# A new stored order for the 1722 operations of an attention and gMLP kernel

## The chip, the core and the metric

One of the eight cores of a Trainium2 chip runs the whole program. A core has five engines, each with a queue of its own that it works through strictly in order: PE (TensorE, the matrix multiplier), ACT (ScalarE, activations), DVE (VectorE), POOL (GpSimd) and SP (SyncE, which here only issues DMAs). An engine that reaches an instruction whose inputs are not ready waits, and everything behind that instruction on the same engine waits with it. The metric is the device time of one execution in microseconds (us); lower is better.

## What is computed

The reference takes x (2048 rows of 448 numbers, bf16) and applies two blocks, each with a residual and with a modulation that comes from a vector c:

```
sa, ca, ga, sb, cb, gb = (silu(c) @ w_mod) cut into six
h = layernorm(x) * (1 + ca) + sa
x = x + ga * A(h)
h = layernorm(x) * (1 + cb) + sb
x = x + gb * B(h)
```

A is causal attention with 16 heads of 28 and a window of 256 rows, then a projection with wo. B is a gated MLP: z = gelu(h @ w_in) is halved into z1 and z2 (896 columns each); z2 is normalised over its columns and mixed over all 2048 rows, g = w_sp @ layernorm(z2) + b_sp; the result is (z1 * g) @ w_out.

## The kernel before, in words

**Tiles.** The 2048 rows are 16 tiles of 128, called t or j. Attention runs per tile j over the up to three key tiles kb = j-2, j, j-1, in two halves each, so that there are 90 pairs of a score block and its exponential.

**Operations.** The program is a list of 1722 operations, each made once by a helper (`pe`, `dve`, `pool`, `load`, lines 438 to 448) with its inputs, the buffers that it touches and the engines that may run it. The names that the prediction uses are:

- load and norm of x: `l1_t` is the statistics of tile t (st, ag, ve on DVE, line 588 to 595), `l1_trs` the power of minus one half on POOL (line 596), `xn` the normalised tile (lines 609, 610, 639), `tr` its transpose on PE, `hT` or `hm` the modulation that gives the transposed h (lines 672, 677, 686). `modA` and `modAe` make the modulation's columns (line 573), and `zv` and `zqk` are memsets on POOL that clear rows of weights (lines 526, 527).
- projections: `qk` and `v` on PE, with `qke` (line 785 on DVE, 782 on ACT) and `ve` (797, 794) which copy the result out of PSUM.
- attention: `S` the scores on PE, `E` the exponential on ACT (line 884), `M` the mask on POOL (line 890), `PV` on PE, then `oq`, `rec`, `nrm`, `oT` (lines 916 to 925; oq, rec and oT on DVE, nrm on either of two engines), `wo` on PE and `x1` on DVE (line 935, the residual).
- second norm: `l2_t` and `x2` as `l1` and `xn`, `h2T` a transpose by DMA, `h2m` its modulation (line 686; four of them, c = 0 to 3, serve two tiles, and what reads h waits for all four).
- block B: `z2m` and `z1m` on PE, `z2g` and `z1g` the gelu on ACT (988, 992, 1011), `l3` the statistics of z2, `z2n` its norm on DVE (line 610), `wsp` a transposing DMA of a piece of w_sp, `G` the mixing over rows on PE in four quarters of four matmuls with 512 columns each, `ga` and `gu` on DVE (1080, 1082), `out` on PE, `fin` the last residual on DVE (1102) and `st` the store (1104).

**Order and waits.** The order is not found when the kernel is built. It stands in the text `ORDER` from line 177, one token for an operation: its number, after a dot which of its possible engines runs it, and after a slash which buffers (PSUM banks, SBUF slots) its new tensors get. `schedule` reads the tokens:

```python
        for tok in ORDER.split():
            head, _, picks = tok.partition("/")
            num, _, opt = head.partition(".")
            o = self.ops[int(num)]
            ...
                    t.got = t.options[picks.pop(0)]
            ...
            o.eng, _, o.fn = o.opts[int(opt or 0)]
            ...
            self.order.append(o)
```

So the order of the tokens of one engine is the order of that engine's queue. A buffer that is used again makes its new user wait for all users of the old tensor. `emit` then writes each queue with the semaphore waits that the inputs and the reused buffers demand; the order between engines comes from these waits alone. `column_tiles` looks at runs of certain PE operations: those that stand next to a column-tiled one are themselves run as four matmuls of 32 columns (line 453 in place of line 456).

**The PSUM banks.** There are eight. The scores use three pairs (0 and 1, 2 and 3, 4 and 5) in the early part, and the rest of attention works with banks 4 to 7 one at a time; a projection, a wo or a z2m that takes a bank waits until DVE or ACT has emptied it. In block B all eight banks are in use.

Of the kernel before, what the change touches and what calls it, by code (L numbers as in the profile page):

```python
# [177 lines left out]
22 23 1 0 33 32 3 19 26 1700/0 20 30 1701 21 31 34/0 35 36 1702 1703 1704 1705 2 5 6 62 63 24 64 25 65 66/1 71/7 69/0 73/6 1706 1707 9 37/2 38 39 40  # L178
41 29.1 13 42 43 4 67/3 44 45 1708 1709 1710 46 47 48 49 50 51 52 53 72 1711 1712 1713 1714 1715 1716 60.2 70.1 74 1717 120 121 122 123 85/2 1718 68.1
175 61.1 75/6 76 90/0 91 10 124 177 54.2 1719 1720 1721 110/5 111 86 87 80/4 92 93 176 77 57.1 78 178 56.1 79.1 58 88 81 82 83 179 125.2/4 128/1 94 89  # L180
126/0 112 59 113 84 491/0,0 129 160/1 161 12 8 17 127.1 162 150/0 151 152 114 140/3 141 180 493/8 155/2 142 156 157 163 164 240 55.2 16 143 244 181
242 246 153 154 183.2/4 100/0 101 95/2 102 103 96 97 98 105/3 158 159 243 245 104 241 130/1 131 132 133 134 182.1/2 184/0 106 185 99 247 144 248 249
28.1 186.1 323 250 251/3 254.1/0 11 145/2 146 147 148 149 327 107 108 109 252.1/1 329 135/1 136 137 328 138 139 492/0,0 496/0 494 115/1 116 7 117 118
119 165/2 166 167 168 170/0 171 187/3 169 188 508/1,0 253.1/2 325 512/7 189.1 172 173 174.1 489/2 513 200/3 201 202 203 15 509/1 510 204 190/1 191 192
193 194 210/0 515/1,0 516/4 518/3 195/3 27 211 212 213 326 220/1 221 222 223 14 490 205/2 206 207 208 209 214.1 495/0 497 224.1 498 196 330 324 331
499/0 500 215/1 216 217 18 408 332 255 218 219 529/0,1 530/8 235/0 197 198 533/0 258 199.1 409 225/2 226 227 228 229.1 501.1/0 256 257 261.1 236 237
238 333 262 259 260 230/3 239 231 232 233 536/1,0 514/0 511 234 335/2 537/9 406 407 263/2 264 265 283/3 284 540/10 336.1/1 531 303/1 266 267 285 286
# [984 lines left out]
```

## Time and profile before

Three runs gave 271.55, 272.40 and 272.97 us, so a median of 272.40 us. The profiled execution took 271.84 us, of which the trace's span is 270.1 us; the other 1.7 us lie around it.

| | busy us | share of the span |
|---|---|---|
| PE, matmuls | 257.9 | 95% |
| PE, weight loads (beside the matmuls) | 127.5 | 47% |
| DVE | 175.4 | 65% |
| ACT | 132.9 | 49% |
| POOL | 98.6 | 37% |

The granted TensorE clock is full in every slice of the profile. The time falls into four stretches: the start (0 to about 17 us: loads, the modulation, the first norm and projections); attention (to about 108 us, the last scores), in which ACT works through the 90 exponentials while PE does scores, PV, projections and the first of block B; the rest of z1 and z2 (to about 147 us); and the dense stretch, in which PE does G and out, to the last store.

A line of the chain of waits names a time in us, a length, an engine and what it did; it is followed back from the last instruction. A group line ends with the idle time of the engine ahead of that group, and who ended it.

### The profile page before, as it was taken

Reading aid. Unit: us, or ns where it says so; the run is one execution under the profiler, and the core shown is the slowest. Engines: PE = TensorE matmul, PEld = TensorE weight load, DVE = VectorE, ACT = ScalarE, POOL = GpSimd, SP = SyncE. Lnnn points to the kernel's source line nnn. Section 1 sums busy time; section 2 is a strip of 40 time slices with the busy share of each in tenths; the row PEclk is TensorE's granted clock in tenths of the full one; section 3 lists DMA queues with packets and bytes.
Section 4 is the critical chain, followed back from the end, with each engine's and each line's share of the span. In section 5 each row is a group of like instructions: output and inputs, shape, how many; then the busy total and the mean of one; then the engine's idle time right before and its main releaser. Section 6 shows DMA issues by size and latency. Waiting matters only on the chain.

```text
span 270.1 us, 7271 instructions
## 1 busy us (share of the span) xinstructions
PE 257.9 (95%) x3128; PEld 127.5 (47%) x3149; DVE 175.4 (65%) x414; ACT 132.9 (49%) x180; POOL 98.6 (37%) x158
## 2 busy tenths in 40 slices
PE   6889999999999989999999999999999999999995
PEld 2657444554455443454444444444444444444453
DVE  3899798978989989698987944341334233332443
ACT  4789999999999998967687200001000000000000
POOL 3577377766888678753731210000000000000000
PEclk9999999999999999999999999999999999999999
DMA  7975335350579851957699990000000000000013
GB/s 226 379 176 55 65 86 90 98 136 4 127 107 221 119 80 22 157 100 156 134 152 188 194 175 21 0 0 2 0 0 0 2 0 34 34 2 34 17 51 106
DMA packets 60862, 23.97 MB, mean 89 GB/s; under 512 B 49822, under 2 KB 60701, under 8 KB 60829
## 3 DMA queue, kind: packets, MB, share of 16 engines
q1 hardware_dynamic: 60555, 23.03, 41.9%
q8 instruction: 25, 0.41, 0.6%
q10 hardware_dynamic: 274, 0.46, 0.5%
q14 instruction: 8, 0.07, 0.1%
HBM read 9.59 MB, written 1.84 MB: 42 GB/s over the span
## 4 chain that ended last, share of the span: by engine, by line
PE 77%; DVE 15%; DMA 3%; issue 1%; ACT 1%; POOL 1%; DVEq 0%; ACTq 0%; SPq 0%
PE ps L456 71%; PE ps L453 6%; DVE st_all L588 2%; DVE QKT L785 2%; DVE oq L916 2%; DMA wmod_sb<-in_w_mod_dram 2%; DVE w_out_sb L940 1%; DVE oT L925 1%; DMA out_dram<-fin 1%; DVE hT L686 1%; DVE x_sb L935 1%; DVE z L982 1%; ACT PT L884 1%; DVE o_sb L921 1%; DVE mv_all L591 1%
## 5 line engine op out<-in xcount | busy, mean ns | idle before, releaser
L884 ACT ACTIVATE PT<-ps 128x1024 bf16<-128x1024 f32 x90 | 85.0, 1038 | 3.3 <-PE ps L456 3.0
L1080 DVE TENSOR_TENSOR tmpg<-ps,bsp_bc 128x512 bf16<-128x512 f32 x28 | 19.4, 692 | 59.7 <-PE ps L456 56.8
L456 PE MATMUL ps<-QKT,z 128*128 128x512 bf16 x218 | 49.9, 379 | 0.3
L890 POOL TENSOR_SCALAR_AFFINE_SELECT PT<-PT 128x512 f32<-128x512 f32 x60 | 37.0, 638 | 10.5 <-ACT PT L884 10.4
L1011 ACT ACTIVATE z1T<-ps 128x512 bf16<-128x512 f32 x28 | 15.1, 596 | 39.1 <-PE ps L456 39.0
L456 PEld LDWEIGHTS ps<-QKT,z 128*128 128x128 bf16 x224 | 21.8, 98 | 26.4 <-ACT z2raw L992 0.4
L596 POOL TENSOR_TENSOR rs_all<-ve_all,neghalf 128x1 f32<-128x1 f32 (+2 forms) x30 | 20.1, 673 | 32.6 <-DVE ve_all L595 32.5
L456 PE MATMUL ps<-w_spC,z 128*128 128x512 bf16 x111 | 25.4, 379 | 0.1
L456 PE MATMUL ps<-w_spD,z 128*128 128x512 bf16 x110 | 24.7, 379 | 0.1
L456 PE MATMUL ps<-w_out_sb,z1T 128*128 128x448 bf16 (+2 forms) x119 | 22.3, 341 | 0.1
L456 PE MATMUL ps<-w_in_sb,hT 128*128 128x448 bf16 (+1 forms) x101 | 22.0, 353 | 0.0
L456 PE MATMUL ps<-hT,w_in_sb 128*128 128x512 bf16 (+1 forms) x87 | 20.9, 380 | 0.5 <-ACT z1T L1011 0.2
L588 DVE BATCH_NORM_STATS2 st_all<-z2raw 128x6 f32<-128x448 bf16 x32 | 18.7, 613 | 1.4 <-ACT z2raw L992 0.8
L588 DVE BATCH_NORM_STATS2 st_all<-x_sb 128x6 f32<-128x448 bf16 x32 | 19.2, 612 | 0.5 <-DMA x_sb<-in_A_x_dram 0.3
L456 PE MATMUL ps<-hT,WQK 128*128 128x128 bf16 (+2 forms) x109 | 18.2, 295 | 1.3 <-DVE oq L916 0.3
L456 PE MATMUL ps<-QKT 28*128 28x128 bf16 x720 | 18.3, 217 | 0.8 <-DVE hT L677 0.5
L785 DVE CAST QKT<-ps 128x512 bf16<-128x512 f32 (+2 forms) x26 | 16.1, 623 | 3.5 <-PE ps L456 2.4
L609 POOL TENSOR_SCALAR xn<-x_sb,rs_all,nm_all 128x512 bf16<-128x512 bf16 x20 | 15.7, 787 | 4.1 <-DVE nm_all L600 3.1
L456 PEld LDWEIGHTS ps<-w_spC,z 128*128 128x128 bf16 x112 | 10.9, 98 | 13.2 <-ACT z2raw L992 0.2
L456 PEld LDWEIGHTS ps<-w_spD,z 128*128 128x128 bf16 x112 | 11.0, 98 | 13.0
L456 PEld LDWEIGHTS ps<-QKT 28*128 28x128 bf16 x720 | 10.4, 92 | 13.9 <-ACT PT L884 10.1
L456 PEld LDWEIGHTS ps<-w_out_sb,z1T 128*128 128x128 bf16 x119 | 11.5, 98 | 10.1 <-DVE z1T L1082 0.4
(90 smaller groups left out, 331.8 us busy)
## 6 DMA issues: line engine op xcount, KB each, us to landing
wmod_sb<-in_w_mod_dram SPq DMA_DIRECT2D x8, 224.0 KB, 3.6
w_in_sb<-in_B_w_in_dram SPq DMA_DIRECT2D x8, 224.0 KB, 2.9
out_dram<-fin SPq DMA_DIRECT2D x16, 112.0 KB, 1.7
x_sb<-in_A_x_dram SPq DMA_DIRECT2D x3, 448.0 KB, 7.3
wqk_raw<-in_A_wqkv_dram SPq DMA_DIRECT2D x2, 452.0 KB, 6.0
bsp_bc<-in_B_b_sp_dram SPq DMA_DIRECT2D x1, 512.0 KB, 6.2
wmod_sb<-in_w_mod_dram SPq DMA_DIRECT2D x1, 448.0 KB, 4.9
wmod_sb<-in_w_mod_dram ACTq DMA_DIRECT2D x1, 448.0 KB, 5.0
```

The lines of the kernel that those rows point to most:

```text
L453: last = e.matmul(out_[32 * j:32 * j + 32], lhsT=lhsT[:, 32 * j:32 * j + 32], rhs=rhs, start=st, stop=sp, tile_position=(0, 32 * j), **kw)
L456: return e.matmul(out_, lhsT=lhsT, rhs=rhs, start=st, stop=sp, **kw)
L588: st = [dve("%sst%d" % (name, i), prio, dve_ns(D), lambda e, i=i, s_=s_: e.bn_stats(st_all[:, slot, t, i, :], s_()), deps, tens) for i, s_ ...
L591: return dve(name + "ag", prio, 100, lambda e: e.bn_aggr(mv_all[:, slot, t, :], st_all[:, slot, t, 0:n, :]), st)
L596: r = pool(name + "rs", prio, 420 + 148 * n, lambda e: e.tensor_tensor(rs_all[:, slot, t0:t1], ve_all[:, slot, t0:t1], neghalf[:, t0:t1], ...
L609: return e.tensor_scalar(dst, src, rs_all[:, slot, t:t + 1], nm_all[:, slot, t:t + 1], ALU.mult, ALU.add)
L785: return e.tensor_copy(QKT[:, g, cols], ps[:, ten.slot, 0:w])
L884: e_op = P.op("E%d_%d" % (j, ui), pr, [("act", 925, lambda e, e_in=e_in, e_out=e_out: e.activation(e_out(), e_in(), ACT.Exp, scale=SCALE)) ...
L890: ready = pool("M%d_%d" % (j, ui), pr - 50, pool_ns(512), lambda e, pt=pt, pat=pat, cm=cm, cmp=cmp: e.affine_select(out=pt32(pt.slot), in_ ...
L916: tq = dve("oq%d" % j, pr - 10, dve_ns(512), lambda e, pv_ten=pv_ten, qt=qt: e.transpose(out=oq[:, qt.slot, :], in_=ps[:, pv_ten.slot, :]) ...
L1011: g = P.op("z1g%d_%d" % (tb, ft), pr - 19, [("act", act_ns(512), lambda e: e.activation(z1T[:, ft, tb * 512:(tb + 1) * 512], ps[:, ten.slo ...
L1080: a = dve("ga%d_%d" % (tb, ft), pr, dve_ns(512), lambda e, tb=tb, ten=ten, tg=tg: e.tensor_tensor(tmpg[:, tg.slot, :], ps[:, ten.slot, :], ...
```

## The change

Only the text `ORDER` changes. The operations, their inputs and the code that reads the order stay as they are; line numbers behind the text go up by one, since the new text is one line longer. It was found by a search that replays the order with assumed durations, in three versions, two of which disturb the durations and the DMA latencies.

```diff
 ORDER = """
-22 23 1 0 33 32 3 19 26 1700/0 20 30 1701 21 31 34/0 35 36 1702 1703 1704 1705 2 5 6 62 63 24 64 25 65 66/1 71/7 69/0 73/6 1706 1707 9 37/2 38 39 40
...
-1566 1567/3 1568 1675/3 1676 1677 1678 1679/3 1680 1635/2 1636 1637/0 1638 1573/3 1574 1575/0 1576 1685/2 1686 1687/3 1688 1578 1689/7 1690 1691/2
-1681/2 1682 1683/0 1623/5 1624 1625/1 1684 1692 1696/0 1697 1626 1693/4 1694 1698/3 1695 1699 1579/2 1580 1569/5 1570 1571/0 1572
+13 23 20 31 0 33 1 26 22 32 3 30 34/0 35 19 1700/0 25 1701 21 1702 1703 36 1704 62 63 1705 24 64 65 2 5 6 61.1 1706 1707 9 66/0 73/3 69/6 67/0 71/4
...
+1690 1691/2 1568 1577/7 1578 1579/1 1580 1685/4 1686 1692 1687/1 1688 1696/6 1697 1698/3 1693/1 1573/2 1574 1575/2 1576 1694 1695 1699 1569/0 1570
+1571/0 1572
 """
```

Read through the list of operations, it does this. Forty operations change their engine: 21 go from DVE to POOL (among them hm4_0, hm4_3, hm5_0, hm5_3, nrm1, nrm5, x2_0, x2_11 and ten of the h2m), 10 from POOL to DVE (nrm7, nrm8, x2_9, x2_12 and others), 4 from ACT to DVE (hT0_2, qke2_5, qke3_2, ve4), 4 from DVE to ACT (hT0_0, hT0_1, hT2_1, z2e4_1), 1 from ACT to POOL. DVE has 400 operations where it had 411, POOL 166 where it had 154, ACT 175 where it had 176 (two of them DMAs); PE 871 and SP 110 in both. The waits in the five queues go from 961 to 957. Column-tiled operations go from 246 to 250, and PE's changes of tile shape from 120 to 119. On PE the scores keep their order and their distance from each other: ahead of each S up to S15_4 stands the same PE work within half a microsecond. Within that the queues are reordered in hundreds of places. The places that the prediction speaks of, as they stand in the queues (an engine in brackets where the operation moved there):

```
POOL, start
 before  wqkf0_0  l1_2rs  wqkf0_1  xn2  l1_4rs  zv  xn7
 after   wqkf0_0  wqkf0_1  xn2  zv  l1_4rs  xn7
DVE, start
 before  xn0  zwp  modAe  hT0_1  l1_1st0  l1_1ag  l1_1ve  hT0_0  l1_2st0
 after   xn0  l1_1st0  l1_1ag  modAe  l1_1ve  hT0_2  l1_2st0
DVE, before v10 on PE
 before  qke4_2  hm5_0  hm5_2  x1_5  qke4_7
 after   qke4_2  hm5_2  rec6  x1_5  qke4_7            (hm5_0 is on POOL)
DVE, before qk5_1 and wo7 on PE
 before  qke5_5  l2_5st0  l2_2nm  x2_0  qke5_3  x1_6  l2_6st0  qke5_1  oT7  l2_4st0  l2_4ag  l2_5ag  qke5_0
 after   qke5_5  qke5_3  l2_4ve  x1_6  qke5_1  oT7  l2_6st0  qke5_0
DVE, second norm of tiles 12 and 13
 before  oq14 rec14 nrm14 h2m8_2 oT14 l2_12st0 l2_12ag l2_13ag l2_12ve z2e4_0 ... x1_14
 after   oq14 l3_7st1 l2_13st0 rec14 nrm14 l2_12ag l3_7st0 oT14 z2e4_0 x1_14 l2_13ag l2_12ve
POOL, the same
 before  M15_3  l2_12rs  x2_13  l3_7rs
 after   M15_3  l2_12rs  h2m8_1  h2m8_0  h2m10_2  h2m10_0  x2_13  h2m10_1  h2m10_3
last outs on PE
 before  ... out13  out7  out14  out12  out8  outh15  out15  out5
 after   ... out4  out12  out14  out7  out13  outh15  out15  out6  out5
slots of the four fin buffers that the last fins take, and whose store must have landed first
 before  fin7 takes that of fin14 (st14), fin5 that of fin12 (st12)
 after   fin13 takes that of fin7 (st7), fin6 that of fin14 (st14), fin5 that of fin12 (st12)
```

SP's queue changes too: wv0, one half of the v weights, is the 8th load on it and was the 13th, and the 32 wsp pieces come in another order (10 of them ahead of h2T15, where it was 14).

113 lines of the change are left out of this document (57 added, 56 removed).

## The prediction

> **What bounds the kernel now.** I read the page first (busy times, slices), then the busy time by stretch, then the chain of waits in order of time, and last the timelines of single engines around each gap of the chain. On the page, the digits are tenths of a fortieth of the span.
>
> ```profile
> span 270.1 us, 7271 instructions
> PE 257.9 (95%) x3128; PEld 127.5 (47%) x3149; DVE 175.4 (65%) x414; ACT 132.9 (49%) x180; POOL 98.6 (37%) x158
> ACT  4789999999999998967687200001000000000000
> L884 ACT ACTIVATE PT<-ps 128x1024 bf16<-128x1024 f32 x90 | 85.0, 1038 | 3.3 <-PE ps L456 3.0
> ```
>
> PE is busy nearly everywhere, but a busy PE in the trace is not yet a full one, so I look at who is full beside it. ACT is at nine tenths or more from 20 to 105 us: there it sets the pace with its 90 exponentials, and all that it could still give is the 3.3 us that it stood idle ahead of them, 3.0 of them for PE. After attention ACT empties and PE alone counts:
>
> ```profile
> 70.00:80.00 10.00, 9.41 (x251) 4.99 (x251) 9.08 (x22) 9.71 (x12) 8.94 (x15) 1.00 0.75 110
> 160.00:170.00 10.00, 9.95 (x47) 4.54 (x47) 4.64 (x8) 0.00 (x0) 0.00 (x0) 1.00 0.22 44
> ```
>
> (Columns: PE, weight loads, DVE, ACT, POOL, granted clock, DMA share, GB/s.) From 160 us on PE lacks 0.05 us in ten. The chain shows the same stretch as matmuls end to end, and PE's timeline the last of them:
>
> ```profile
> 162.74 10.74 PE ps L456 x49
> ```
>
> ```profile
> 255.43 11.34 PE L456 MATMUL ps<-w_out_sb,z1T 128*128 128x448 bf16 x66
> ```
>
> 49 matmuls in 10.74 us are 0.219 us each, and the last one ends at 266.77. The amount of PE work is the same before and after, so the dense stretch cannot become shorter; it can only begin earlier or later, or get holes. The end is thus: the time at which PE leaves attention, plus a constant, plus holes in what follows, plus the tail behind the last matmul. The sum goes by these four.
>
> **Term 1, the start: -0.45 us.** The columns below are start, length, engine and line; the bracket is the idle time ahead of it and its releaser.
>
> ```profile
> 7.85 0.17 DVE L573 TENSOR_TENSOR modT<-ps,zero_one 128x8 f32<-128x8 f32 x1 [2.23 <-PE ps L456]
> 8.38 0.62 DVE L588 BATCH_NORM_STATS2 st_all<-x_sb 128x6 f32<-128x448 bf16 x1
> 16.36 0.29 PE L456 MATMUL ps<-QKT 28*128 28x128 bf16 x8 [0.54 <-DVE hT L677]
> 16.91 0.93 PE L456 MATMUL ps<-wv_sb,hT 128*128 128x448 bf16 x4 [0.27 <-POOL wv_sb L526]
> 15.43 1.01 POOL L596 TENSOR_TENSOR rs_all<-ve_all,neghalf 128x4 f32<-128x4 f32 x1 [0.76 <-DVE ve_all L595]
> 16.39 0.46 POOL L526 MEMSET wv_sb<- 64x448 bf16 x1
> ```
>
> The v projection starts at 16.91 because zv ends at 16.85, and zv starts late only because it stands behind l1_4rs (1.01 us). In the new order it stands ahead of that, right after xn2; POOL was idle for 0.76 there, in which its 0.46 fits. So v0 follows the scores S0_0h2 directly, which end at 16.65, and 0.27 of idle PE go. S0_0h2 itself waits 0.54 for hT2_0 on DVE, which has as many statistics ahead of it as before; a little comes of the rest of the start, and I give it 0.1. Behind v0, hT2_1 leaves DVE, where v1 and gateA were ahead of it in time and qk2 on PE waited on, for ACT:
>
> ```profile
> 19.17 1.02 ACT L884 ACTIVATE PT<-ps 128x1024 bf16<-128x1024 f32 x1 [0.57 <-PE ps L456]
> ```
>
> ACT was idle for 0.57 ahead of this exponential, E1_1, so hT2_1, shorter than an exponential, costs it 0.4 at most and mostly nothing. For qk2's earlier start I give 0.08. That makes 0.27 + 0.1 + 0.08 = 0.45. A loss stands against this: modAe (the 7.85 row) is now behind the statistics of tile 1 (the 8.38 row), whose x must have landed.
>
> ```profile
> x_sb<-in_A_x_dram SPq DMA_DIRECT2D x2, 112.0 KB, 3.8
> DMA to landing us min/median/max: 2.0/6.2/8.3
> ```
>
> ```profile
> 9.40 0.32 DVE hT L677
> ```
>
> The two 112 KB loads have a median of 3.8 us and the shortest is 2.0, so the second takes some 5.6; issued some 2.2 us after the start (SP's fourth issue) it lands at 7.8. Statistics (0.62) and their aggregate come first, so modAe ends near 8.77 in place of 8.02: 0.75 late. Before, the last of the four hT0 ended at 9.72 (the 9.40 row), behind these same statistics on DVE. Now one is on DVE and three on ACT, one after the other, from 8.8: at 0.3 to 0.4 each the last ends near 9.95. So the first projections lose some 0.25, and the wait for hT2_0 at 16.36 swallows it. Ends for this term: -0.9 (the 0.54, the 0.27 and the 0.1) and +0.5 (0.75 less 0.25, if nothing swallows it).
>
> **Term 2, attention: -0.7 us.** Two of the chain's stalls on DVE lie where ACT was waiting for scores.
>
> ```profile
> 56.76 0.25 DVE rec_all L917
> ```
>
> ```profile
> 59.82 1.33 DVE hT L686 x2
> 61.15 0.54 DVE x_sb L935
> ```
>
> ```profile
> 69.63 0.53 DVE st_all L588
> 70.16 0.06 DVE nm_all L600
> 70.22 0.67 DVE xn L609
> 70.89 0.61 DVE QKT L785
> 71.54 0.83 PE ps L453 x12
> ```
>
> In the first, v10 on PE waits for x1_5 (61.15) to empty its bank, and that stands behind hm5_0 and hm5_2, 1.33 us for the two. hm5_0 goes to POOL and rec6 comes in (a reciprocal took 0.25): x1_5 is ready 1.33/2 - 0.25 = 0.41 us sooner. In the second, qk5_1 (the 71.54 row) waits for qke5_3 (70.89), and between qke5_5 and qke5_3 stand l2_5st0, l2_2nm and x2_0, 0.53 + 0.06 + 0.67 = 1.26 us, all gone from there. What PE has to gain stands in the list of waits (total, times, longest):
>
> ```profile
> PE ps L456 <- DVE x_sb L935: 0.6, 2, 0.3
> ...
> PE ps L453 <- DVE QKT L785: 0.4, 2, 0.3
> ```
>
> One of each is here: 0.3 + 0.3 = 0.6. Whether time comes of it depends on ACT:
>
> ```profile
> 63.62 8.75 ACT L884 ACTIVATE PT<-ps 128x1024 bf16<-128x1024 f32 x9 [0.20 <-PE ps L456]
> 72.54 1.94 ACT L884 ACTIVATE PT<-ps 128x1024 bf16<-128x1024 f32 x2 [0.17 <-PE ps L456]
> ```
>
> ```profile
> 103.08 3.93 ACT L884 ACTIVATE PT<-ps 128x1024 bf16<-128x1024 f32 x4 [0.57 <-PE ps L456]
> 107.52 1.02 ACT L884 ACTIVATE PT<-ps 128x1024 bf16<-128x1024 f32 x1 [0.51 <-PE ps L456]
> ```
>
> Two exponentials in a row take 1.94, one alone 1.04 (the group's mean), so they start 0.90 apart. Nine at that pace take 8 x 0.90 + 1.04 = 8.24; the row at 63.62 takes 8.75, so 0.51 lie inside it, and with 0.20 and 0.17 ahead ACT has 0.88 to give. Between PE's 0.6 and ACT's 0.88 I take 0.7. The 0.57 and 0.51 at the end of attention stay: PE has the same work between the scores there. Ends: 0 and -3.3 (the whole idle time of the group).
>
> POOL gets hm5_0, hm5_3, nrm5 and x2_0 between 55 and 80 us and gives up nrm7: three operations more, at most 1.01 each (the longest POOL row above), where it has 8.94 of ten in the second half. I cost that at +0.2, as a mask is needed only when its PV comes, behind the next scores; without that cover it costs up to 3.0.
>
> **Term 3, from attention to the last matmul: +0.2 us.** Here PE had no gap over 0.2, and I see none closing. It can get one: l2_12ve now stands behind x1_14 on DVE, and on POOL l2_12rs, which waits for it, has h2m8_1 and h2m8_0 behind it, without which z2m9 cannot start.
>
> ```profile
> 116.15 1.32 PE ps L453 x24
> ```
>
> ```profile
> 115.67 0.70 POOL L596 TENSOR_TENSOR rs_all<-ve_all,neghalf 128x2 f32<-128x2 f32 x1 [2.61 <-DVE ve_all L595]
> 117.59 0.61 DVE L935 TENSOR_TENSOR x_sb<-ps,x_sb 128x448 bf16<-128x448 f32 x1
> 119.06 1.09 POOL L686 TENSOR_SCALAR hT<-hT,modT 128x256 bf16<-128x256 bf16 x2
> ```
>
> x1_14 (117.59) ends at 118.2; with an aggregate and l2_12ve (0.3) then l2_12rs (0.70) and two modulations (1.09) h2m8_0 ends at 120.3. PE ends wo14 at 117.47 (the 116.15 row) and comes to z2m9 at about 120.7, counting the 12 matmuls of 0.2 and the six PV of some 0.1 that now stand between. So 0.4 us to spare; I charge half of a miss of that size, +0.2. The G part starts with the same four quarters ahead of the first that needs z2n4, and the first that needs z2n12 to z2n15 comes one quarter (0.86) later than before. z1m3_6, the changed banks and the 32 wsp pieces I cost at nothing: the first pieces that G needs are issued ahead of or soon after h2T15, and DVE is at 4.64 of ten. Without that cover G waits for its piece, for as long as the longest landing shown, 8.3. The four more column-tiled operations: 12 matmuls, three operations, take 0.83 in the 71.54 row, so 0.28 at most against 0.22; four times 0.06, beside ACT's exponentials. Ends: 0 and +2.8 (below).
>
> **Term 4, the tail: -0.5 us.**
>
> ```profile
> 266.77 1.16 DVE L1102 TENSOR_TENSOR fin<-ps,x_sb 128x448 bf16<-128x448 f32 x2 [0.86 <-DMA out_dram<-fin]
> ```
>
> The last out ends at 266.77 (the 255.43 row), but DVE was held by fin7, which waited for a store to free its slot, and fin5 starts only when fin7 is through, half of the 1.16 later: 0.54, as their overlap is small. In the new order the store in the way is st7, in front of fin13, two outs earlier; finh15, fin6 and fin15 catch up behind it before the last out ends. So fin5 starts at once: -0.54, with the ends 0 and -0.54.
>
> **Sum.** -0.45 - 0.7 + 0.2 + 0.2 - 0.5 = -1.25. Against the profiled execution's own 271.84 us (span 270.1) that is 270.6; that execution lies 0.56 under the median of the runs shown, 272.40, and against that it is **271.1 us**, which I give. About 0.5%, 1.36 us, is what a measurement of this kernel can tell from no change.
>
> **The rivals.** *Handover late (slower).* The place is DVE's and POOL's queue between x1_14 and z2n4: DVE is in order, each norm waits for a power on POOL, and the new order puts l3_7ve, l2_12ve and others behind operations with other waits. POOL already stood idle there for want of a DVE result once, 2.61 us ahead of the 115.67 row. If the new order makes one such wait fall on what PE needs next, PE has nothing else to run and stops as long: 271.1 + 2.6 + 0.3 (the two h2m10 behind it, less the slack) = **274.0 us**. It decides from 2.7 us of lateness, where it eats the gain and 0.5% more. For it: a slack of 0.4 us. Against it: the same idle row says that POOL has room to catch up there.
>
> *The DVE time comes back (no change).* A modulation that went to POOL takes DVE's time all the same, if DVE waits for POOL:
>
> ```profile
> 27.46 0.72 DVE L610 TENSOR_SCALAR xn<-x_sb,mv_all,rs_all 128x512 bf16<-128x512 bf16 x1
> 31.18 0.38 DVE L610 TENSOR_SCALAR xn<-x_sb,mv_all,rs_all 128x512 bf16<-128x512 bf16 x1
> ```
>
> The same norm took 0.72 us with POOL at work and 0.38 with POOL waiting. With 0.34 more on two of each three of the 12 operations that POOL gains net, DVE loses 2.7 us, two thirds of them in attention, and term 2 and half of term 1 are gone: 272.4 - 0.5 - 0.2 + 0.2 = **271.9 us**. The Trainium skill, "SBUF — State Buffer", section "Who interferes with whom", says that a VectorE operation in a two-port mode and a GpSimd operation exclude each other for a whole instruction. The two rows agree with it; by that rule this rival is the outcome.
>
> *More closes.* The order may also close the gaps that I left: half of what is left of the 3.3 us ahead of the exponentials, 1.3, the whole start, 0.45, and no cost on POOL, 0.2: 271.1 - 1.95 = **269.1 us**. For it: wo11, v15 and z2m2 have shorter DVE work in front in some places. Against: the 1.08 at S15.
>
> **How the numbers follow.** My forecast of 271.1 (its own range 270.3 to 271.9) 0.38; more closes, 269.1, 0.18; the DVE time comes back, 271.9, 0.20; handover late, 274.0, 0.24. Faster by over 0.5% means under 271.04: 0.18, 0.19 of the forecast's 0.38 and 0.03 of the third case, so 0.40. Slower means over 273.76: of the 0.24 about 0.20, and 0.03 for a start that loses its 0.5 with anything else, so 0.23. The rest, 0.37, is no change. The range takes the likelier half of either side: 268.7 (269.1 and 0.4 more of the idle) to 274.1.
>
> **What would show it.** Right: no idle ahead of v0 that POOL's wv_sb ends; the scores of tiles 8 and 9 come 0.4 to 0.8 earlier; ACT's idle time ahead of L884 (L885 then) falls from 3.3 to about 2.4; the last fin starts as the last out ends. Wrong: a PE wait for DVE hT or POOL hT at 118 to 125 us, a PE wait for DVE z just after G begins, more idle ahead of the exponentials, or a first hT0 after 10 us that moves everything behind it.

## The result, and the profile after

The changed kernel takes 271.0 us (median of 16 runs, 270.61 to 271.88); the kernel before, timed beside it, 272.63 us (median of 16, 271.55 to 274.8). The ratio is 0.9942, with a 95% interval of 0.9923 to 0.996: 0.58% faster. The profiled execution took 270.71 us with a span of 268.7 us, so the two profiled spans lie 1.4 us apart.

These are lines of the page of the changed kernel (busy times, the slices of ACT, the exponentials). Line numbers have gone up by one.

```profile
span 268.7 us, 7296 instructions
PE 256.8 (96%) x3139; PEld 127.5 (47%) x3161; DVE 172.5 (64%) x402; ACT 133.3 (50%) x180; POOL 106.6 (40%) x170
ACT  4889999999999998966786200000000100000000
L885 ACT ACTIVATE PT<-ps 128x1024 bf16<-128x1024 f32 x90 | 84.6, 1044 | 2.9 <-PE ps L457 2.8
```

POOL has 8.0 us more to do, DVE 2.9 less. ACT's idle time ahead of the exponentials has fallen from 3.3 to 2.9 us. The same two stretches by engine show PE as before: 9.95 of ten once attention is over.

```profile
70.00:80.00 10.00, 9.61 (x305) 5.63 (x310) 8.47 (x21) 9.88 (x12) 8.86 (x15) 1.00 1.18 220
160.00:170.00 10.00, 9.95 (x48) 4.51 (x47) 2.92 (x5) 0.00 (x0) 0.00 (x0) 1.00 0.45 101
```

So what counts is when the stages begin and end. The table gives the times at which single operations end in the two traces (when their semaphore shows it), in us.

```
                                    before    after   difference
first matmul of v0                   17.29    16.63      -0.66
scores S1_0                          19.14    19.01      -0.14
scores S4_0                          38.75    38.58      -0.17
scores S4_2                          41.10    40.55      -0.55
scores S8_0                          61.46    60.93      -0.53
scores S8_4                          65.55    64.43      -1.12
scores S11_0                         78.66    77.44      -1.22
scores S15_0                        103.06   101.70      -1.36
scores S15_4                        107.50   106.32      -1.18
last out matmul                     266.78   265.83      -0.95
last fin                            267.94   266.50      -1.44
```

Read downwards: the start gives 0.14, attention 1.04 more (0.38 near 40 us, 0.59 near 63, 0.10 from there to S11_0, 0.14 from there to S15_0, and at the end 0.18 back), 0.23 is lost between attention and the last out, and the tail gives 0.49. I take the parts in this order.

**Start.** The chain of waits in order of time now begins so:

```profile
2.22 5.50 DMA x_sb<-in_A_x_dram
7.73 0.64 DVE st_all L589
9.62 0.48 DVE nm_all L627
10.12 0.82 ACT xn L640
```

In the kernel before it began with the load of the modulation weights and PE's work on them:

```profile
1.34 4.99 DMA wmod_sb<-in_w_mod_dram
6.37 1.46 PE ps L456 x36
```

**Attention.** ACT's timeline of the changed kernel has one unbroken row from 39.5 to 74.1 us, in which the kernel before stood idle three times (0.28, 0.20 and 0.17 us); at the end of attention the gaps are still there.

```profile
39.52 34.62 ACT L885 ACTIVATE PT<-ps 128x1024 bf16<-128x1024 f32 x37
...
101.72 1.94 ACT L885 ACTIVATE PT<-ps 128x1024 bf16<-128x1024 f32 x2 [0.51 <-PE ps L457]
103.89 1.94 ACT L885 ACTIVATE PT<-ps 128x1024 bf16<-128x1024 f32 x2 [0.23 <-PE ps L457]
106.34 1.02 ACT L885 ACTIVATE PT<-ps 128x1024 bf16<-128x1024 f32 x1 [0.51 <-PE ps L457]
```

**Behind attention.** PE's timeline has a new hole, ahead of z2m7, and DVE's timeline shows the three modulations (h2m6) that it waits for: 1.84 us for three.

```profile
107.97 1.60 PE L457 MATMUL ps<-w_in_sb,hT 128*128 128x448 bf16 x8 [0.35 <-DVE hT L687]
```

```profile
106.07 1.84 DVE L687 TENSOR_SCALAR hT<-hT,modT 128x256 bf16<-128x256 bf16 x3
```

**Tail.** DVE's timeline: the wait for a store has moved forward, the fin that waited and three more follow in a row, and the last fin starts 0.03 us after the last out matmul ends at 265.83.

```profile
263.48 1.90 DVE L1103 TENSOR_TENSOR fin<-ps,x_sb 128x448 bf16<-128x448 f32 x4 [2.31 <-DMA out_dram<-fin]
265.86 0.62 DVE L1103 TENSOR_TENSOR fin<-ps,x_sb 128x448 bf16<-128x448 f32 x1 [0.48 <-PE ps L457]
```

### The profile page after: what moved, and what is told of

Same layout as the page of the kernel before. It is cut to its first block, busy times and chain, and to the rows that moved or that the text cites. A ratio compares the mean times of both kernels' runs of the same rounds, so it can differ in the third digit from the quotient of the medians.

```text
span 268.7 us, 7296 instructions
## 1 busy us (share of the span) xinstructions
PE 256.8 (96%) x3139; PEld 127.5 (47%) x3161; DVE 172.5 (64%) x402; ACT 133.3 (50%) x180; POOL 106.6 (40%) x170
## 3 DMA queue, kind: packets, MB, share of 16 engines
HBM read 9.59 MB, written 1.84 MB: 43 GB/s over the span
## 4 chain that ended last, share of the span: by engine, by line
PE 81%; ACT 8%; DVE 7%; DMA 2%; issue 1%; SPq 0%; DVEq 0%
PE ps L457 72%; PE ps L454 8%; ACT PT L885 7%; DMA x_sb<-in_A_x_dram 2%; DVE st_all L589 1%; DVE hT L687 1%; DVE w_out_sb L941 1%; DVE hT L678 1%; DVE oq L917 1%; DVE x_sb L936 0%; DVE z L983 0%; DVE nm_all L627 0%; SPq L484 0%; ACT xn L640 0%; DVE o_sb L922 0%
## 5 line engine op out<-in xcount | busy, mean ns | idle before, releaser
L891 POOL TENSOR_SCALAR_AFFINE_SELECT PT<-PT 128x512 f32<-128x512 f32 x60 | 37.8, 646 | 7.7 <-ACT PT L885 7.5
L786 DVE CAST QKT<-ps 128x512 bf16<-128x512 f32 (+2 forms) x28 | 17.2, 616 | 3.4 <-PE ps L457 1.9
L687 POOL TENSOR_SCALAR hT<-hT,modT 128x256 bf16<-128x256 bf16 (+1 forms) x28 | 17.6, 636 | 3.3 <-DMA hT<-xn 3.3
L457 PE MATMUL ps<-hT,WQK 128*128 128x128 bf16 (+2 forms) x108 | 17.2, 298 | 1.3 <-issue 0.6
L610 POOL TENSOR_SCALAR xn<-x_sb,rs_all,nm_all 128x512 bf16<-128x512 bf16 x21 | 17.0, 815 | 2.7 <-DVE nm_all L601 1.9
L1103 DVE TENSOR_TENSOR fin<-ps,x_sb 128x448 bf16<-128x448 f32 (+2 forms) x17 | 10.0, 596 | 11.9 <-PE ps L457 7.8
```

The source lines that it names most:

```text
L457: return e.matmul(out_, lhsT=lhsT, rhs=rhs, start=st, stop=sp, **kw)
L610: return e.tensor_scalar(dst, src, rs_all[:, slot, t:t + 1], nm_all[:, slot, t:t + 1], ALU.mult, ALU.add)
L687: return e.tensor_scalar(hT[:, c_, cols], hT[:, c_, cols], modT[:, base_col + 4 + c_:base_col + 5 + c_], modT[:, base_col + c_:base_col + ...
L786: return e.tensor_copy(QKT[:, g, cols], ps[:, ten.slot, 0:w])
L891: ready = pool("M%d_%d" % (j, ui), pr - 50, pool_ns(512), lambda e, pt=pt, pat=pat, cm=cm, cmp=cmp: e.affine_select(out=pt32(pt.slot), in_ ...
L1103: fs.append(dve("fin%s%d" % (nm, t), pr, dve_ns(c1 - c0), lambda e, t=t, ten=ten, ft_=ft_, c0=c0, c1=c1: e.tensor_tensor(fin[:, ft_.slot, ...
```

## The experiments

All twelve are edits of the text `ORDER` (in one, of a mask as well). Medians are of 6 to 12 runs each, and the ratio is against the kernel before, timed in the same series. The effects sought are 0.1 to 0.5 us, while single runs of the kernel before lie over 2 us apart, so most verdicts rest on the traces. They allow it: where two kernels have the same order, their operations keep their distance to some 0.05 us over long stretches; where they do not, the text says so. "From the same start" means that the difference at the scores S1_0 has been taken off.

### att: three moves in attention, on the kernel before

```diff
-547 415 416 571/2,1 574/3
+547 415 571/2,1 574/3
-548/0 549 288/1 289
+548/0 549 416 288/1 289
-639 422 425 427 381/1
+639 422 425.1 427 381/1
-727 461 984 462 927
+727 461 462 927
-666 667 973 959.1/0 733/0 739/0,2 463.1 439/1 440
+666 667 733/0 739/0,2 463.1 984 973 959.1/0 439/1 440
```

> The kernel before with three moves only: l1_12nm goes behind oq2 and rec2 on DVE, hm5_0 goes from DVE to POOL, and l2_5st0, l2_2nm and x2_0 go behind qke5_3. Theory (each of the three stalls of PE on DVE closes by itself, and the exponentials keep the time): the exponential after S4_2 comes 0.25 us earlier than before, those of tile 8 some 0.7, those from the middle of tile 9 on some 0.95; first 38 us and tail as before; span 270.1 - 0.95 = 269.15. Rival (a gap that closes opens another behind it, so that only the whole new order gains): a gap goes, but the last exponential of attention is within 0.3 us of before, and the span is 269.8 to 270.4.

Median 272.62 us (271.44 to 273.67), ratio 1.0003 (0.9982 to 1.0023); the profiled span is 270.5. S1_0 is 0.90 later than in the trace of before, by a chance that the kernel "warm" below takes up. From the same start S4_2 is 0.39 earlier and S8_2 0.76, as expected of the first two moves; but S10_0 only 0.11, and the last scores of attention, S15_4, too. PE's and ACT's timelines show where the third move lost it:

```profile
72.98 0.30 PE L456 MATMUL ps<-PT,Vaug 128*32 128x128 bf16 x8 [0.79 <-DVE x_sb L935]
```

```profile
73.33 2.85 ACT L884 ACTIVATE PT<-ps 128x1024 bf16<-128x1024 f32 x3 [0.83 <-PE ps L456]
```

Behind qke5_3 the three operations stand ahead of x1_6, which empties the bank for the next PV. So both held: two stalls close by themselves, and the third only changes its place unless the three operations are put where nothing waits.

### tail: one store issued sooner, on the kernel before

```diff
-1690 1691/2 1681/2 1682
+1690 1691/2 1692 1681/2 1682
-1625/1 1684 1692 1696/0 1697
+1625/1 1684 1696/0 1697
```

> The kernel before with one move only: the store st14 is issued right behind fin14, ahead of st12, instead of behind it on SP's queue. Theory (fin7 waits for st14 to free its slot, and st14 is late because SP waits for fin12 first): fin7 starts without the 0.86 us wait for the store, the last fin starts within 0.1 us of the end of the last matmul, span 270.1 - 0.5 = 269.6. Rival (the slot is reused too soon whatever the queue does, by the time that a store takes): DVE still waits for the store ahead of fin7, span 270.0 to 270.2.

Median 272.33 us (271.25 to 273.6), ratio 0.9992 (0.9971 to 1.0013). The profiled span is 270.8, not 269.6, since this execution has a late start (S0_0h0 ends at 13.55 in place of 12.55). In its trace the last out matmul ends at 267.98, and DVE's timeline shows the last fin without any wait for a store:

```profile
268.00 0.62 DVE L1102 TENSOR_TENSOR fin<-ps,x_sb 128x448 bf16<-128x448 f32 x1 [0.37 <-PE ps L456]
```

From there to the end of the fin it is 0.66 us; in the trace of before it was 1.16. The theory holds for that trace: st14 stood on SP behind st12, which waits for a later fin. The median shows less than 0.5 (0.31, with an interval that takes in no change), and the other traces with the old tail say why. DVE's timeline of "att", and below it of "stats1st":

```profile
267.18 1.16 DVE L1102 TENSOR_TENSOR fin<-ps,x_sb 128x448 bf16<-128x448 f32 x2 [0.50 <-DMA out_dram<-fin]
```

```profile
267.20 0.62 DVE L1102 TENSOR_TENSOR fin<-ps,x_sb 128x448 bf16<-128x448 f32 x1 [0.16 <-PE ps L456]
```

The same store took 2.91 us from issue to landing in the trace of before, 2.54 in "att", 2.52 in "warm" and 2.15 in "stats1st", and from the last out matmul to the end of the last fin it was 1.16, 0.78, 0.77 and 0.66 us. The old tail costs 0.5 us in one of four traces, 0.1 in two, nothing in one.

### zvback: zv behind l1_4rs again, on the changed kernel

```diff
-243 14 28.1 247 245 248 249 185 186.1
+243 14 247 245 248 249 28.1 185 186.1
```

> The changed kernel with zv back behind l1_4rs on POOL. Theory (the gain at v0 is real but is lost again ahead of E1_1): v0 comes 0.2 to 0.3 us later than in the changed kernel with an idle time ahead of it that POOL's wv_sb ends, E1_1 within 0.1 us, span 268.6 to 268.8. Rival (v0's start carries through to the end, as the prediction had it): E1_1 and everything behind it 0.25 us later, span 268.95.

Median 270.88 us (270.51 to 271.97), ratio 0.9948 (0.9928 to 0.9967); span 268.8. The idle time ahead of v0 is back:

```profile
16.75 0.93 PE L457 MATMUL ps<-wv_sb,hT 128*128 128x448 bf16 x4 [0.32 <-POOL wv_sb L527]
```

v0 ends 0.49 later than in the changed kernel, S1_0 0.11, and S0_0h0, before any of it, 0.10. So of v0's 0.39 nothing is left one stage on. PE's timeline of the changed kernel shows why: there PE waits behind v0 instead, for an exponential, and in "zvback" this wait is gone.

```profile
17.45 0.28 PE L457 MATMUL ps<-ident,xn 128*128 128x128 bf16 x2 [0.27 <-ACT PT L885]
```

The theory holds: within the new order that part of the change is worth nothing.

### hT2dve: hT2_1 on DVE again, on the changed kernel

```diff
-508/0,1 323 189 512/1 173
+508/0,1 323 189.1 512/1 173
```

> The changed kernel with hT2_1 back on DVE, at its new place. Theory (the v projection starts 0.66 us earlier, but only 0.1 of it reaches the exponential E1_1, since hT2_1 now stands ahead of that on ACT): E1_1 comes 0.2 to 0.4 us earlier than in the changed kernel, and as ACT is full behind it, the span falls by as much, to 268.3 to 268.5. Rival (E1_1 waits for its scores, whatever ACT does, or DVE brings hT2_1 later and qk2 waits): E1_1 or the exponentials of tile 2 are not earlier, span 268.6 to 269.1.

Median 271.35 us (271.03 to 272.11), ratio 0.9956 (0.9938 to 0.9974); span 269.9. My theory falls. From the same start (S1_0 is 0.21 later) S1_2 is 0.44 later and S2_0 0.62, and this stays until S10_0; 0.24 more is lost by S10_4, and at the end it is 1.01. Where the later losses come from stays open. PE's timeline, before it the same work in the changed kernel:

```profile
19.87 1.36 PE L457 MATMUL ps<-hT,WQK 128*128 128x256 bf16 x11
```

```profile
20.51 1.38 PE L457 MATMUL ps<-hT,WQK 128*128 128x256 bf16 x11 [0.27 <-DVE hT L678]
```

qk2 waits for hT2_1, which DVE brings later than ACT did. So within the new order hT2_1 on ACT saves 0.62 us in the traces and is not a cost. The medians lie only 0.35 apart (271.35 and 271.0): the profiled execution of "hT2dve", 271.96, is at the slow end of its runs.

### warm: the warm-up matmuls in one row, on the kernel before

```diff
-19 26 1700/0 20 30 1701 21 31 34/0 35 36
+19 26 20 31 34/0 1700/0 30 1701 21 35 36
-1704 1705 2 5
+1704 1705 1706 1707 2 5
-69/0 73/6 1706 1707 9 37/2
+69/0 73/6 9 37/2
```

> The kernel before with one move only: on PE the four c_cols matmuls stand ahead of all warm-up matmuls, and the first eight warm-up matmuls then stand in a row, as in the changed kernel. Theory (in most executions of the kernel before the tempo of PE's matmuls doubles only after some 10 us, as its warm-up has gaps, and the profiled execution of before was one of the lucky ones): the warm-up matmuls of 256 columns take 0.27 us on average, the scores S0_0h0 end at 12.4 to 12.8, the median falls from 272.64 to 271.7 to 272.0, and the highest time comes down to some 272.8. Rival (the late starts of the two kernels of the first series come from something else, landings or chance): S0_0h0 is as scattered as before, and the median is 272.4 to 272.9.

What made me ask: three traces with the old start (before, "att" and "tail") have the end of S0_0h0 at 12.55, 13.49 and 13.55 us, though wmodA0, wmodA1, wqk1, x0b and x1 land 0.15 to 0.4 us sooner in "tail" than in the trace of before. The difference is PE. These are the warm-up matmuls of 256 columns in the group view of the first 12 us (count, total, mean in ns), of before and of "att":

```profile
L456 PE MATMUL ps<-warm 128*128 128x256 bf16 x13 | 2.1, 273 | 0.0
```

```profile
L456 PE MATMUL ps<-warm 128*128 128x256 bf16 x13 | 3.2, 382 | 0.0
```

In "att" and "tail" PE still runs at half tempo while it works on modA, and modA's end moves the whole start. The granted clock does not show it; this is the row of "att" for 7 to 9 us, where the clock, the third number from the end, stands at 1.00:

```profile
7.00:9.00 2.00, 2.00 (x26) 1.41 (x25) 0.50 (x3) 0.34 (x1) 1.33 (x2) 1.00 1.07 391
```

The Trainium skill, "TensorE: Matmul & The Clock Gate", section "Part 1: The HAM clock gate", says that PE runs at half its clock until it has been busy for about 3.4 us, watched in a window that runs free of the kernel, so that the point of change varies from run to run. The traces agree that it varies, but 3.4 us is no fixed mark in them. The change shows in how far apart matmuls of 512 columns start: 0.43 us before it, 0.22 behind it. Eight warm-up matmuls in a row come in eight traces, "warm", the changed kernel and its variants without "oldwarm"; the change falls between 5.7 us ("x29late", 2.7 us behind the start of the row) and 7.5 to 8.2 us ("zvback", over 4.6 us behind it). With the old warm-up (two, then six with gaps) it came before modA or in its beginning in the traces of before, "few" and "oldwarm", and only behind it, after 9 us, in "att", "tail" and "stats1st".

"warm" has a median of 272.17 us (271.87 to 273.12), ratio 0.9987 (0.9972 to 1.0002). The mean is 275 ns, as the theory had it, and the highest time is lower than that of the kernel before in that series (273.75). But S0_0h0 ends at 13.11. PE's timeline of "warm" shows two reasons:

```profile
2.92 3.59 PE L456 MATMUL ps<-warm 128*128 128x512 bf16 x8
6.63 0.56 PE L456 MATMUL ps<-sc_sb,wmod_sb 128*128 128x1 bf16 x14
7.26 0.78 PE L456 MATMUL ps<-warm 128*128 128x512 bf16 x3
```

The row of eight keeps PE from modA (the x14) until 6.63, where the kernel before began it at 6.37. And modA begins at half tempo here too: the three warm-up matmuls behind it take 0.59 us in the trace of before, 1.01 in "att" and 0.78 here, so the change came among them. The last modA ends at 8.38, against 7.83 in the trace of before. So the tempo is one source of the scatter, and one row in place of the old warm-up does not cure it in this trace; the lower median of the theory did not come.

### x29late: x2_9 behind the modulations h2m6, on the changed kernel

```diff
-1327 1316 1021.1/1 1329 835
+1327 1316 1329 835
-1009 1010 1180/2 1182
+1009 1010 1021.1/1 1180/2 1182
```

> The changed kernel with x2_9 behind the last of the three modulations h2m6 on DVE, instead of in front of them. Theory (the idle 0.35 us of PE ahead of z2m7 is a real part of the cost behind attention): the modulations end 0.3 us or more earlier, the idle time goes, and everything behind it, the end too, is 0.3 us earlier, counted from the same start of S0_0h0. Rival (x2_9's transposition lands later by the 1.7 us and z2m9 waits instead, or the next operation takes the gap): wo15_3 and the end are within 0.1 us, or later.

Median 270.83 us (270.71 to 271.23), ratio 0.9937 (0.9918 to 0.9956); span 268.8. The idle time ahead of z2m7 is gone (from wo13 on z2m7 comes 0.47 earlier), 0.17 of it comes back behind it, yet at the end the trace shows nothing, since 0.33 had been lost ahead of it. That loss is worth a look: DVE's timelines of the changed kernel and of this one, and POOL's of this one:

```profile
98.01 0.38 DVE L610 TENSOR_SCALAR xn<-x_sb,rs_all,nm_all 128x512 bf16<-128x512 bf16 x1
```

```profile
98.10 1.24 DVE L610 TENSOR_SCALAR xn<-x_sb,rs_all,nm_all 128x512 bf16<-128x512 bf16 x1
```

```profile
98.25 0.94 POOL L922 TENSOR_TENSOR o_sb<-oq,rec_all 128x448 bf16<-128x448 f32 x1
```

Nothing is changed at this place. Up to there this execution runs 0.07 later, on DVE 0.09. In the seven other traces of the new order POOL's nrm12 begins 0.166 to 0.180 us behind x2_7, and x2_7 takes 0.38; here it begins 0.153 behind. By that x2_7 seems to have missed its turn: instead of being done in 0.38 us ahead of POOL's nrm12, it ends at 99.35, just after nrm12 (99.20). A difference of 0.01 to 0.03 us between DVE and POOL goes with 0.86 us more for x2_7 and 0.3 for PE. That it decided the turn is read from these lengths; no run sets it.

### nomask: three masks left out on POOL, on the changed kernel

```diff
-                ready = pool("M%d_%d" % (j, ui), pr - 50, pool_ns(512), lambda e, pt=pt, pat=pat, cm=cm, cmp=cmp: e.affine_select(
+                ready = pool("M%d_%d" % (j, ui), pr - 50, pool_ns(512), (lambda e, pt=pt: e.memset(pt32(pt.slot)[:, 0, 0:8], 0.0)) if (j, ui) in (
+                    (14, 2), (14, 3), (15, 2)) else lambda e, pt=pt, pat=pat, cm=cm, cmp=cmp: e.affine_select(
```

> The changed kernel without three masks on POOL (M14_2, M14_3, M15_2: the masking of the scores of three pairs of blocks is left out, a memset of eight columns stands in its place), so that POOL rests while DVE does the three modulations h2m6. Theory (a modulation on DVE takes 0.58 us in place of 0.26 to 0.34 because POOL works at the same time): the three take 0.26 to 0.34 each, 0.7 us less together, PE's idle 0.35 us ahead of z2m7 goes, and the end is 0.3 us earlier from the same start. Rival (their length has nothing to do with POOL): they take 0.55 to 0.6, and the end is within 0.1 us.

Median 270.6 us (270.25 to 271.2), ratio 0.9931 (0.9909 to 0.9954). DVE's timeline has the three modulations in 0.85 us in place of 1.84:

```profile
106.36 0.85 DVE L687 TENSOR_SCALAR hT<-hT,modT 128x256 bf16<-128x256 bf16 x3
```

From the same start h2m6_2 ends 0.98 earlier, z2m7 comes 0.47 earlier, 0.17 comes back as in "x29late", and the last fin is 0.30 earlier. The theory holds: the hole ahead of z2m7 is made by POOL's masks, beside which DVE ends a modulation every 0.58 us instead of every 0.26. This is the rule of the Trainium skill that the prediction cites ("SBUF — State Buffer", "Who interferes with whom"), and the rows agree with it.

### x0bearly: x0b loaded ahead of wqk1, on the changed kernel

```diff
-65 2 5 6 61.1 1706
+65 2 6 5 61.1 1706
```

> The changed kernel with the load x0b issued ahead of wqk1 on SP. Theory (the start hangs on x0b's landing at 7.7 us, since modAe stands behind the statistics of tile 1): x0b lands some 0.5 us earlier, modAe ends 0.3 us earlier (then PE's modA matmuls end last), S0_0h0 and all behind it are 0.3 us earlier, and the median falls from 271.0 to 270.7. Rival (wqk1, which now lands 0.3 us later, holds ACT or POOL, and with them hT0): S0_0h0 is not earlier, median 270.9 to 271.3.

Median 271.23 us (270.85 to 272.25), ratio 0.9951 (0.9933 to 0.9969). x0b lands at 6.60 in place of 7.71 and modAe ends 0.67 earlier, but S0_0h0 ends 0.40 later. The chain of waits has gone over to the other load:

```profile
2.21 5.62 DMA wqk_raw<-in_A_wqkv_dram
...
7.87 0.85 POOL wqk_raw L528
...
9.39 0.53 POOL rs_all L597
```

The rival held: POOL works on wqk1 first, and the power that the norm of tile 1 needs stands behind that.

### stats1st: the statistics of tile 1 ahead of modAe, on the kernel before

```diff
-51 52 53 72
+51 52 120 121 53 72
-74 1717 120 121 122 123
+74 1717 122 123
```

> The kernel before with one move only: l1_1st0 and l1_1ag stand ahead of modAe on DVE, as in the changed kernel. Theory (the start hangs on the norm of tile 1; the statistics of tile 1 ahead of modAe bring it sooner, and PE's tempo in its first 8 us no longer matters, since modA then has time to spare): S0_0h0 ends 0.5 us or more earlier than in the kernel before (12.0 to 12.2 us, against 12.55 to 13.55 in the three executions traced with the old start), this carries to the end, the median falls by 0.5 to 1.2 us to 271.2 to 271.9, and the highest times come down. Rival (as the prediction had it: modAe 0.75 us later is a loss, which the wait for hT2_0 at best swallows): S0_0h0 is not earlier, and the median is 272.3 to 273.0.

Median 272.82 us (271.78 to 274.4), ratio 1.0006 (0.9985 to 1.0028). Its span, 271.9, is long for a reason of its own: from the end of the last fin to the end of the span it has 4.03 us, while the 13 other traces have 2.17 or 2.18. In its trace PE doubled its tempo late and S0_0h0 ends at 13.00; in "few", with the same start and an early doubling, it ends at 12.67, against 12.55 in the trace of before. So modAe 0.57 later costs some 0.12, as far as one trace of each can tell, and what is gained on the norm (l1_1nm 0.31 earlier) is lost on ACT, whose timeline has three copies of the weights ahead of that norm:

```profile
9.32 1.66 ACT L710 ACTIVATE WQK<-wqk_raw 128x512 bf16<-128x512 bf16 x3
10.88 0.80 ACT L639 ACTIVATE xn<-x_sb,nm_all,rs_all 128x512 bf16<-128x512 bf16 x1
```

The theory falls, as far as one move goes. In the changed kernel ACT makes two of these copies while it waits for modAe, others are on POOL, and the same norm starts at 10.12.

### few: the moves that the traces point to, on the kernel before

```diff
-51 52 53 72
+51 52 120 121 53 72
-74 1717 120 121 122 123
+74 1717 122 123
-547 415 416 571/2,1 574/3
+547 415 571/2,1 574/3
-548/0 549 288/1 289
+548/0 549 416 288/1 289
-639 422 425 427 381/1
+639 422 425.1 427 381/1
-933 958 706 961/2 453.1 682
+933 958 984 706 961/2 959/0 453.1 682
-727 461 984 462 927
+727 461 462 927
-667 973 959.1/0 733/0 739/0,2
+667 973 733/0 739/0,2
-1690 1691/2 1681/2 1682
+1690 1691/2 1692 1681/2 1682
-1625/1 1684 1692 1696/0 1697
+1625/1 1684 1696/0 1697
```

> The kernel before with seven operations moved: l1_1st0 and l1_1ag ahead of modAe; l1_12nm behind rec2; hm5_0 to POOL; l2_5st0 behind l2_0nm, x2_0 to POOL behind x2_1, so that of the three only l2_2nm is left ahead of qke5_3; st14 behind fin14. Theory (the gain of the new order comes from these places): from the start of S0_0h0 on, the scores S4_2 come 0.39 us earlier, those of tile 8 0.75, S10_0 1.0, the last fin 1.5; with the start 0.5 us or more earlier the median is 270.3 to 270.8, as good as the changed kernel or better. Rival (the places were only one outcome of the whole order, other waits take them back as in the first series): the last fin is less than 1.0 us earlier from the same start, median 271.2 or more.

Median 271.41 us (270.5 to 272.42), ratio 0.9951 (0.9932 to 0.997); the profiled span is 268.8, that of the changed kernel 268.7. From the same start S4_2 comes 0.36 earlier, S8_2 0.74, S10_0 1.07, the last out 1.05 and the last fin 1.54. ACT's timeline has no gap in 40 exponentials:

```profile
39.09 37.32 ACT L884 ACTIVATE PT<-ps 128x1024 bf16<-128x1024 f32 x40
```

Seven operations moved give in the trace the 1.04 of attention and the 0.49 of the tail that the whole new order gave, without its loss of 0.23 behind attention. The median says less: it is 0.41 above that of the changed kernel, where the rival had put it, and the profiled execution is the fastest of the twelve. The start did not get its 0.5 us.

### masks: x2_9 later and two masks sooner, on the changed kernel

```diff
-1327 1316 1021.1/1 1329 835
+1327 1316 1329 835
-1009 1010 1180/2 1182
+1009 1010 1021.1/1 1180/2 1182
-1351/3 1020 902 871/0 868 877 881 1352
+1351/3 1020 877 874 902 871/0 868 881 1352
-1022 883 874 875 884/0
+1022 883 875 884/0
```

> The changed kernel with x2_9 behind the three modulations h2m6 and with the masks M14_3 and M14_2 ahead of M15_2 on POOL, into the 1.5 us in which POOL stood idle. Theory (what made PE wait ahead of z2m7 is DVE sharing its time with POOL, and the waits behind z2m7 take back 0.17): the idle time ahead of z2m7 goes, and the end is 0.3 us earlier from the same start of S0_0h0; median 270.6 to 270.8. Rival (the masks now hold DVE's other operations of that stretch, which are of the same kind): no change from the changed kernel, median 270.9 to 271.1.

Median 271.28 us (270.38 to 271.66), ratio 0.9937 (0.9913 to 0.9962). The part in question does what it should: h2m6_3, 1 and 2 end 0.26 us apart, and between S15_4 and wo15 0.30 are gained (0.86 late against 0.56 late), of which 0.14 are lost again by the last out. But this execution had become 0.8 late between 74 and 85 us, where nothing is changed; one of the places is this, in which PE waited for nothing that the profile shows:

```profile
80.52 0.76 PE L457 MATMUL ps<-PT,Vaug 128*32 128x128 bf16 x39 [0.38 <-issue]
```

From six runs the median says neither for nor against: inconclusive as a better version.

### oldwarm: the old warm-up, on the changed kernel

```diff
-33 1 26 22
+33 1 19 26 22
-3 30 34/0 35 19 1700/0 25 1701 21 1702
+3 30 1700/0 1701 34/0 35 25 21 1702
-6 61.1 1706 1707 9 66/0
+6 61.1 9 66/0
-67/0 71/4 37/1 38
+67/0 71/4 1706 1707 37/1 38
```

> The changed kernel with the warm-up of the kernel before: the memset of the warm tile stands ahead of that of Vaug on POOL, two warm-up matmuls stand ahead of c_cols, four behind it, and two behind the first transpositions of xn0. Theory (the changed kernel's times lie closer together and its median is 0.2 to 0.3 us better than the profiled executions tell, because its warm-up matmuls stand in one row and PE doubles its tempo before modA in every execution): with the old warm-up some executions double their tempo late, the times scatter over more than 2 us, as in the kernel before, the median rises to 271.2 to 271.8 and the highest lies above 272.3; in a profiled execution of the late kind the warm-up matmuls of 256 columns take more than 0.3 us on average. Rival (the start of the new order hangs on x0b's landing and has room for a slow PE): median 270.8 to 271.1, spread as in the changed kernel, 1.3 us.

Median 270.97 us (270.56 to 272.36), ratio 0.9947 (0.9928 to 0.9967). The scatter is wider (1.8 us against 1.27), the median is that of the changed kernel. So the warm-up does not make its gain. That the new start has room for a slow PE is argued: the profiled execution doubled its tempo in the beginning of modA (mean 272 ns), so no trace has the old warm-up, the new start and a PE that is slow to the end of modA. Nearest is "zvback", where PE was still at half tempo when the last 24 matmuls of modA began (7.48 us): modA ended 0.36 later than in the changed kernel, S0_0h0 only 0.10. And in all seven traces with the new start and x0b at its place, S0_0h0 ends 4.14 to 4.19 us behind the landing of x0b, whatever PE's tempo. That landing is what the new start hangs on, until, with x0b moved ahead ("x0bearly"), wqk1 takes its place.

## Why the prediction was right, step by step

The prediction gave 271.1 us, and on the basis of the profiled executions -1.25 us; 271.0 us and -1.44 us of span were measured. The sum came out; its terms did so only in part, and some of the agreement is luck: what the start lacks (0.31) and the stall that I missed (0.38) nearly cancel. The medians lie 1.63 apart where I had forecast 1.25, and that 271.1 is still so close to 271.0 is luck too: the three runs of before that I started from had a median of 272.40, where the longer series has 272.63.

- **Start, -0.45: mis-sized, and made of the wrong pieces.** In the two traces it is worth 0.66 at v0 and 0.14 one stage on. The 0.27 for zv is real at v0 and worth nothing behind it ("zvback"). The 0.08 for hT2_1 on ACT had the wrong reason: qk2's scores S2_0 come only 0.10 earlier than before, and what the move does is to avert a loss of 0.62 that the new order would have without it ("hT2dve"). modAe is 0.61 late, where I had put 0.75, and this is hidden, but not by the wait for hT2_0: even S0_0h0 is 0.66 earlier, because the chain no longer runs over modAe but over the norm of tile 1, whose factors (l1_1nm) come 0.53 earlier. And I took the profiled execution of before for one with a typical start: with the old order it varies with PE's tempo in the first 8 us (S0_0h0 at 12.55 to 13.55 in three traces), with the new one it hardly does (11.77 to 12.17 in seven traces, "x0bearly" left out), and what varies there is the landing of x0b.
- **Attention, -0.7: right in place and size, with one stall missed.** The exponentials behind the first stall come 0.31 and then 0.13 earlier, those behind the second 0.27: 0.71 together. Missed was the same pattern at 39 us: l1_12nm no longer stands ahead of oq2, and S4_2 comes 0.38 earlier ("att", from the same start: 0.39). "att" shows that the stall at 39 us and the first one each hang on a single move, and "few" that the second closes if l2_5st0 and x2_0 go to a place where nothing waits.
- **POOL's three operations, +0.2: the size by luck, the place and cause not as told.** Between 55 and 80 us, where I had put it, the exponentials lose at most 0.02. From S15_0 to S15_4 0.18 are lost, because wo13 waits 0.32 us for oT13. PE ends the last PV13 at 100.43, and from 100.46 to 102.71 DVE runs oq13, rec13, nrm13 and oT13 end to end; none of them waits for POOL, and nrm13, with POOL at work beside it, takes 0.73 us where it took 0.63. So in this stretch POOL's load explains 0.11 of the wait at most; what POOL does to DVE ahead of it was not tried.
- **Behind attention, +0.2: right size, wrong place.** The cost is 0.23. z2m9, for which I had feared, gets h2m8_0 at 119.06, starts at 119.28 (I had said 120.7) and does not wait; the hole is ahead of z2m7, ten us sooner, and "nomask" shows its cause: masks on POOL beside modulations on DVE.
- **Tail, -0.5: right for the profiled execution, too large for most.** 0.49 in the two traces and 0.50 in "tail". But the wait depends on how long one store takes, and in three other traces with the old tail it cost 0.12, 0.11 and 0.
- **Rivals.** The late handover did not come: no wait for DVE or POOL at 118 to 125 us. The DVE time that comes back is a true mechanism (the 1.84 us above), but small on the whole: the 386 operations that are on DVE in both kernels take 0.6 us longer together, by their rows in the two traces, where the rival had 2.7. "More closes" has the missed stall for it.
- **What would show it.** The scores of tiles 8 and 9 came 0.37 to 0.59 earlier than those ahead of them, and the last fin starts as the last out ends, as said. ACT's idle time fell to 2.9, not 2.4; the start's part of the gain is no idle time of that group.

Left open: the medians lie 1.63 us apart, the two profiled times 1.13 (271.84 and 270.71). The larger scatter of the kernel before, from PE's tempo and other chances of the start, would make up the difference, since its profiled execution lies at the fast end both in the start and in the whole time (0.79 below the median, that of the changed kernel 0.29); that it does is argued from the traces, not shown, for each kernel has only one trace. None of the variants is distinctly better than the changed kernel; "nomask" is fastest, but leaves work out.

## What to carry to other kernels

Where an order is tuned to tenths of a microsecond, look for the operation that stands directly ahead of an eviction for which PE waits on a full engine: in the trace of "few" moving four such operations gave all the gain of attention, and "att" shows that the new place must be one where nothing waits. A gap that closes is worth only what is still there one stage on, so follow it to the next wait before adding it to a sum. And a single profiled execution is one draw: ask of each of its waits (a store's landing, PE's tempo at the start) whether the next execution will have it.

## What the runs showed of the hardware

- PE's matmuls run at half tempo at first, while the granted clock reads 1.00: three warm-up matmuls of 512 columns take 1.01 us before the change and 0.59 behind it. With eight warm-up matmuls in a row the change came at 5.7 to 8.2 us in eight traces; with gaps among them it came by 7 us in three and after 9 us in three. Behind the old start this goes with 1.0 us at the first scores (12.55 and 13.55).
- DVE's norms and modulations and POOL's operations take turns, and the loser can wait for a whole operation: 0.38 us became 1.24 beside a POOL operation of 0.94, and modulations ended every 0.58 us in place of 0.26 beside POOL's masks. Which goes first differed between two executions in which the two engines' distance differed by 0.02 us.
- The store st14, the same in each, took from 2.15 to 2.91 us to land in four traces. From the last fin to the end of the span it was 2.17 or 2.18 us in 13 traces and 4.03 in one.
- PE stood for 0.17 and 0.38 us in attention of one execution ("masks") without a wait that the profile shows, at places where the other traces of the new order show none.
